# Two written-out orders of one kernel: the front's list and the round's list of an S4 convolution block

## The chip, the cores and the metric

One core of a Trainium2 chip. The metric is the device time in microseconds of one execution, the median of several.

## The reference

One block of a model on x of 2048 rows and 640 channels, all in float32. The reference, cut to what is computed:

```python
mod = (silu(c) @ w_mod).reshape(c.shape[0], 6, 1, -1)
sa, ca, ga, sb, cb, gb = (mod[:, 0], mod[:, 1], mod[:, 2], mod[:, 3], mod[:, 4], mod[:, 5])
h = layernorm(x) * (1 + ca) + sa
# A: state space convolution, per channel d, N = 128 complex states, L = 2048
P = exp(dt * A)[:, :, None] ** l
K = einsum("dn,dnl,dn->dl", Cc, P, dt * Bc).real
y = irfft(rfft(h, 2 * L) * rfft(K, 2 * L))[:L] + h * D
x = x + ga * y
h = layernorm(x) * (1 + cb) + sb
x = x + gb * ((silu(h @ w1) * (h @ w3)) @ w2)
```

So there are three parts: six modulation vectors from a small matrix product, a long convolution per channel whose kernel K must first be generated, and a gated MLP with a hidden width of 1728.

## The kernel before

The convolution is done as a Fourier transform of two stages, all products on TensorE. The 640 channels are worked in 40 **steps** of 16 channels to generate K and in 5 blocks of 128 channels to convolve; a block has eight groups of frequencies, 40 groups in all, and a word of the convolution with number k works on group k - 10 (LAG = 10), ten steps behind the generation.

The program up to the MLP has three pieces. The **front** (loop in lines 1001 to 1037) runs once over the list FRONT (lines 967 to 993). The **rounds** (loop from line 1054) run 13 times over the list ROUND (lines 1046 to 1052) with the step numbers raised by 4 each time; a word that was done before, in the front or in an earlier round, or that lies outside the steps, is skipped (do, line 918). The **tail** (loop from line 1073) does the last convolution groups, then the MLP follows, bound by TensorE.

A word of a list stands for one operation or a few, and every engine issues its instructions in the order of the words: the wrapper InOrder and keep hold the program order on each engine, and on SP's DMA queue (Qo) in the front. An engine whose next word must wait does nothing else. The words:

- PH: phases on GpSimd (turns, line 571, and a shift, line 575; in the front the shift is a word of its own, PI). AB, CO, SI: absolute value, cosine and sine of the phases, ScalarE.
- PA: two products into PSUM tile pa (line 546), XA: the exponential of it, ScalarE. PQ: four small products into tile pq (line 557), XQ: the exponential of it, ScalarE. In the rounds PA and PQ use the same PSUM bank, B; in the front each names A or B behind a stroke.
- E1, E2, A1, A2: products of exponentials with cosines and sines on VectorE (lines 598, 601, 605, 609). kg: 64 products that sum over the states (line 619). K: its eviction with a scale, VectorE (lines 626, 627). pt: first Fourier stage of K (line 638). uk: its copy to SBUF, ScalarE.
- st: second Fourier stage of a convolution group (line 677, bank A in the rounds). kc: a copy of half of it by ScalarE. T and Y: complex product and sums on VectorE (lines 694, 695, 701, 702). iv: first inverse stage (line 730). zt: every second one is copied by ScalarE and stored to memory.
- In the front: ms, mp, mc, mv (early) and qs, qp, qc, qv (late) are the modulation: sums on TensorE, a copy by VectorE (tile part), a turn on TensorE, columns by VectorE (modT, cols). z and d with a letter or figure prepare the states' parameters. s1 to s4 make the shift of the layernorm, g1 to g3 the gate. ls, lg, lv, ln: sums, power, bias and application of a layernorm to one of 16 row tiles (ln on ScalarE). um: first Fourier stage of such a tile, TensorE. ua, ub: its two evictions, on ScalarE where the word ends in /s (four small products more on TensorE then), else on VectorE. us: the store of it, from one of two buffers. xl, wl, wg, ul: loads, issued by SP.

A figure behind a stroke is the number of **idle products** (warm, line 252) on the identity, written ahead of the word's own products into the same PSUM tile; each has two records in the trace. They keep TensorE busy and compute nothing that is used. Because they write into the word's own tile, they wait until its bank is free. SETS (line 965) says which words need another table of ScalarE's functions; the loop puts the load of a table ahead of the first such word.

```python
def warm(t, n):
    out = t if len(t.shape) == 2 else t[:, 0] if t.shape[2] >= P else t[:, :P // t.shape[2]]
    for _ in range(n):
        Po.matmul(out[:, :P] if len(out.shape) == 2 else out, ident, ident, start=True, stop=True)
```

Of the kernel before, what the change touches and what calls it, by code (L numbers as in the profile page):

```python
# [116 lines left out]
def tile_kernel(ctx: ExitStack, tc: tile.TileContext, a):  # L117
# [4 lines left out]
    us = dram.tile([2, 2, NA, NB, D // 2], F32, name="us")  # L122
# [45 lines left out]
    s1 = kp.tile([P, 2, P], F32, name="s1")  # L168
# [4 lines left out]
    sc = kp.tile([P, KD], F32, name="sc")  # L173
    cT = kp.tile([P, KD], F32, name="cT")
    uk = kp.tile([P, 3, NA, DC], F32, name="uk")
# [11 lines left out]
    r2 = once([P, NA, NB], F32R, "r2")  # L187
    r1 = once([P, NA, NA], F32R, "r1")
    sel = once([P, NA], F32R, "sel")
# [46 lines left out]
    d0 = slice(0, DC)  # L236
    d1 = slice(DC, D)
# [126 lines left out]
    wg = {}  # L364
# [554 lines left out]
    wl = {}  # L919
# [15 lines left out]
    def of(p, name, *args):  # L935
# [29 lines left out]
    SETS = {"x0": 1, "z4": 1, "d5": 1, "XA": 1, "XQ": 1, "zI": 2, "d9": 2, "CO": 2, "SI": 2}  # L965

    FRONT = (
# [24 lines left out]
    ).split()  # L992

    for j in range(4):
# [46 lines left out]
    for i in range(1, 4):  # L1041
# [2 lines left out]
    xp = None  # L1044

    ROUND = (
# [5 lines left out]
    ).split()  # L1052
    in_order[0] = True
    for rnd in range(NS // EB + 3):
# [715 lines left out]
```

## Time and profile before

| | |
|---|---|
| median of 3 runs | 924.53 us (922.68 to 925.52) |
| the profiled execution's own time | 923.54 us |
| its span | 921.7 us, 21031 instructions |
| busy: TensorE, VectorE, ScalarE, GpSimd | 888.2, 699.3, 548.9, 259.6 us |
| front | about 0 to 129.65 us |
| rounds | about 129.65 to 320 us |
| tail of the convolution | about 320 to 367 us |
| MLP | about 367 us to the end |

Times in rows are microseconds from the span's start. PE is TensorE's matmul, PEld its weight load, DVE VectorE, ACT ScalarE, POOL GpSimd, SP the engine that issues most DMAs. A line number is that of the kernel's code, but operations that go through a helper all have the helper's line (L111, L146, L149, L152); there the tile's name tells which word it is. A row of a timeline gives start, duration, engine, line, operation and tiles; a bracket at its end gives the idle time just ahead of it and what ended that. A group row ends in busy time and mean duration, then the idle time ahead of its members and its releaser.

### The profile page before, as it was taken

How to read it: one execution, taken by the hardware profiler on the slowest of the kernel's cores; microseconds unless marked ns; L12 is line 12 of the kernel's file. 1: busy time of each engine (PE TensorE's matmuls, PEld its weight loads, DVE VectorE, ACT ScalarE, POOL GpSimd, SP SyncE). 2: the span in 40 equal slices, each digit the busy share in tenths (PEclk: the TensorE clock that was granted, in tenths of full speed). 3: DMA queues.
4: the chain of work that ended last, by engine and by line, in shares of the span. 5: the costliest groups of instructions: out<-in, count | busy, mean ns of one | idle time of the engine just before them, and what ended most of it. 6: DMA issues, size and time to landing. Idle time of an engine off the chain costs nothing.

```text
span 921.7 us, 21031 instructions
## 1 busy us (share of the span) xinstructions
PE 888.2 (96%) x8461; PEld 693.3 (75%) x8461; DVE 699.3 (76%) x1240; ACT 548.9 (60%) x811; POOL 259.6 (28%) x274
## 2 busy tenths in 40 slices
PE   5999899999999999999999999999999999999998
PEld 3776566677777767688888887778888888888886
DVE  6799888999999978777666665686976666664665
ACT  4799899999999834564334323566543333333432
POOL 3633455454455312132222201221522222100000
PEclk9999999999999999999999999999999999999999
DMA  8755889656666898942131117964322211113452
GB/s 255 238 203 195 258 242 228 168 161 168 165 157 156 215 259 255 262 176 86 58 115 57 58 49 230 284 223 143 100 65 71 81 58 58 58 29 100 146 176 106
DMA packets 109212, 140.87 MB, mean 153 GB/s; under 512 B 20092, under 2 KB 67452, under 8 KB 109116
## 3 DMA queue, kind: packets, MB, share of 16 engines
q1 hardware_dynamic: 103756, 130.30, 48.0%
q0 software_dynamic: 2048, 7.34, 2.3%
q10 hardware_dynamic: 3312, 1.90, 0.7%
q8 instruction: 66, 1.08, 0.5%
q14 instruction: 30, 0.25, 0.1%
HBM read 107.98 MB, written 31.52 MB: 151 GB/s over the span
## 4 chain that ended last, share of the span: by engine, by line
PE 74%; ACT 12%; DVE 9%; issue 2%; DMA 2%; SPq 0%; DVEq 0%; ACTq 0%
PE ps L111 59%; PE p L677 4%; ACT A L146 3%; ACT ph L146 2%; ACT cs L146 2%; PE pz L730 2%; DVE E L598 2%; PE pm L111 2%; ACT L146 2%; PE pt L638 1%; PE pa L111 1%; DVE uk L111 1%; PE pu L111 1%; PE pq L557 1%; ACT kc L149 1%
## 5 line engine op out<-in xcount | busy, mean ns | idle before, releaser
L111 DVE TENSOR_TENSOR s<-ps,s 128x512 f32<-128x512 f32 x138 | 94.9, 687 | 79.7 <-PE ps L111 79.3
L571 POOL TENSOR_TENSOR ph<-thi,iota 128x1024 int32<-128x1024 int32 x40 | 85.9, 2149 | 143.5 <-DVE A L609 95.4
L111 DVE TENSOR_TENSOR gl<-rw,gh 128x640 fp32r<-128x640 f32 x86 | 77.4, 900 | 62.1 <-ACT gh L111 62.1
L111 ACT CAST gh<-rw 128x640 fp32r<-128x640 f32 x86 | 62.5, 727 | 100.2 <-PE ps L111 60.5
L111 POOL TENSOR_TENSOR S<-rw 128x256 f32<-128x256 f32 x46 | 35.9, 782 | 190.6 <-DVE S0l L111 164.4
L111 PE MATMUL ps<-gh,uh 128*128 128x512 f32 x224 | 87.5, 391 | 0.0
L111 PE MATMUL ps<-gl,uh 128*128 128x512 f32 x224 | 87.2, 389 | 0.0
L677 PE MATMUL p<-uk,s 128*64 128x256 f32 x640 | 77.9, 385 | 7.1 <-DVE Y L702 2.3
L111 PE MATMUL ps<-xA,gh 128*128 128x512 f32 x270 | 84.1, 392 | 0.0
L111 PE MATMUL ps<-gh,ul 128*128 128x512 f32 x208 | 81.1, 390 | 0.0
L677 PEld LDWEIGHTS p<-uk,s 128*64 128x64 f32 x640 | 44.6, 136 | 29.5 <-DVE Y L702 3.4
L111 PEld LDWEIGHTS ps<-xA,gh 128*128 128x128 f32 x270 | 50.2, 188 | 12.2 <-ACT gh L111 0.6
L111 PE MATMUL ps<-xA,gl 128*128 128x512 f32 x135 | 52.6, 390 | 0.0
L605 DVE TENSOR_TENSOR A<-A,ph 128x1024 f32<-128x1024 f32 x40 | 51.9, 1297 | 0.0
L598 DVE TENSOR_TENSOR E<-A,cs 128x1024 f32<-128x1024 f32 x40 | 50.1, 1253 | 0.6 <-ACT A L146 0.6
L111 ACT ACTIVATE s<-ps 128x512 f32<-128x512 f32 (+1 forms) x33 | 19.6, 595 | 49.2 <-PE ps L111 47.9
L111 PEld LDWEIGHTS ps<-gl,uh 128*128 128x128 f32 x224 | 42.1, 188 | 9.0
L111 PEld LDWEIGHTS ps<-gh,uh 128*128 128x128 f32 x224 | 42.0, 188 | 8.8
L111 PEld LDWEIGHTS ps<-gh,ul 128*128 128x128 f32 x208 | 39.0, 188 | 8.4
L575 POOL TENSOR_TENSOR ph<-ph,phi 128x512 int32<-128x512 int32 x40 | 44.5, 1114 | 2.5
L730 PE MATMUL pz<-Y,i 64*128 64x128 f32 x640 | 44.4, 278 | 0.3 <-DVE Y L701 0.3
L730 PEld LDWEIGHTS pz<-Y,i 64*128 64x128 f32 x640 | 38.9, 187 | 6.8 <-issue 5.8
(257 smaller groups left out, 2292.9 us busy)
## 6 DMA issues: line engine op xcount, KB each, us to landing
rw<-in_w_dram SPq DMA_DIRECT2D x52, 320.0 KB
us<-u SPq DMA_DIRECT2D x16, 640.0 KB
s<-in_s_dram SPq DMA_DIRECT2D x40, 256.0 KB
i<-in_i_dram SPq DMA_DIRECT2D x40, 256.0 KB
rw<-in_wg_dram SPq DMA_DIRECT2D x31, 320.0 KB
rw<-in_wu_dram SPq DMA_DIRECT2D x28, 320.0 KB
uk<-us SPq DMA_DIRECT2D x32, 256.0 KB
zs<-zt SPq DMA_DIRECT2D x16, 512.0 KB
```

What stands on the lines that cost most here:

```text
L111: ins = fn(*args, **kw)
L146: return tc.keep_in_program_order(S.activation(*args, **kw))
L149: return tc.keep_in_program_order(S.copy(out, in_))
L557: keep(PE.matmul(pQ[s][:, rr, :256], w[r, t, :], bc(sel[r, js], 2, NA) if i else r1[r, js, :], start=(i == 0), stop=(i == 1), tile_positio ...
L571: keep(G.tensor_tensor(p, bc(thi[:, s * SD:s * SD + SD], 2, NPH), bc(iota, 1, SD), op=OP.mult))
L575: keep(G.tensor_tensor(p[:, :, :NA], p[:, :, :NA], bc(phi[:, s * SD:s * SD + SD], 2, NA), op=OP.add))
L598: keep(V.tensor_tensor(EC[s][:, :, 1:3, :], AA[s][:, :, 1:3, :], mid(cs[s]), op=OP.mult))
L605: keep(V.tensor_tensor(A[:, :, 1:3, :], A[:, :, 1:3, :], mid(ph[s]), op=OP.mult))
L638: keep(PE.matmul(pt[c * 64:c * 64 + 64, g, :], kk[:, g, :], s1[:, c, :], start=True, stop=True, tile_position=(0, c * 64)))
L677: keep(PE.matmul(p2[par * 64:par * 64 + 64, pi, c, :], s2[:, pi * 2 + par, c * 64:c * 64 + 64], uk[:, 0:kn + 1:kn, f, :], start=True, stop ...
L730: ins = keep(PE.matmul(pz[:, par, (g % 2) * 2 + pi, :], i1[r, pi, c, :], Y[r, pi, c, :], start=(c == 0), stop=(c == 1), tile_position=(par ...
```

## The change

The front's list gets another order of the same 427 words, with other numbers of idle products (138 for 124 in all), and ub+13 ends in /s now. The round's list gets another order of the same 86 words: E1, kc, kg, T and a sine, with iv and pt, stand at its head, the numbers of its words shift by up to a round accordingly, and idle products stand ahead of other words (8 in a steady round for 5; in all rounds 61 are run for 37). Every word is still done once; nothing else differs. The diff, cut in the front's list:

```diff
@@ -965,30 +965,29 @@
     FRONT = (
...
-        "wg+0 xl+4 zD/1 lv+1 SI+1 wg+1 zE mp+4 mc+3 PA+3/B/7 XA+2 XA+3 mc+4 d0 mv+3 mv+4 s1 PQ+0/A/1 ms+5 "
-        "s2/1 PI+2 ln+1 mp+5 ln+0 xl+6 mc+5 s4 wg+2 ms+6/1 d1 s3 PQ+1/B/1 XQ+0 E1+0 ls+4 um+0/A/1 ls+5 XQ+1 "
-        "ua+0/s ub+0/s um+1/B mv+5 E1+1 ub+1 xl+7 E2+0 PA+4/A/5 d2 ln+2 ua+1 ln+3 PQ+3/B/3 lg+2 XA+4 d3 dC "
-        "us+0 ls+6 ms+7 ls+7 um+2/A mp+6 ua+2 mc+6 lg+3 ub+2/s XQ+3 PQ+2/A/3 um+3/B xl+8 lv+2 ln+5 AB+2 us+1 "
...
-        "ua+12/s pt+2 SI+6 A1+5 uk+2 ub+12 us+12 K+4 um+13/B/2 ub+13 ua+13 ln+15 E2+5 ln+14 A1+6 wl+0 CO+7 "
-        "pt+4/6 PH+8 uk+4 A2+5 um+14/A/1 E2+6 PI+8 us+13 ub+14 wl+1 ua+14 kg+5/2 K+5 PA+8/A/1 PH+9 A2+6 "
-        "um+15/B kg+6/1 wl+2 ua+15 AB+8 SI+7 PH+10 XA+8 qs+0 qp+0 CO+8 pt+3 ub+15 PI+9 qc+0 PA+9/B/4 K+6 SI+8 "
-        "AB+9 E1+7 PQ+8/A/1 qv+0 A1+7 XA+9 qs+1 E2+7 PI+10 XQ+8 AB+10 qp+1 E1+8 PA+10/A/1 qc+1 uk+3 PQ+9/B "
-        "A2+7 XQ+9 E2+8 PH+11 pt+5 qv+1 wl+3 wl+4 XA+10 qs+2 qp+2 kg+7/4 qc+2 A1+8 PI+11 CO+9 CO+10 us+15 "
-        "AB+11 A2+8 qv+2 uk+5 CO+11 PA+11/B E1+9 qs+3 K+7 us+14 pt+7/1 PH+12 qp+3 qc+3 ul+0 qv+3 SI+10 E2+9 "
-        "SI+11 kg+8 qs+4 K+8 PQ+10/A SI+9 uk+7 PI+12 qp+4 A1+9 A2+9 pt+6 XQ+10 qc+4 XA+11 PQ+11/B uk+6 qv+4 "
-        "XQ+11 "
...
+        "x0 r2 z1 sc ld2 z2 z5 z3 z7 zF z8 zG zH z4 zI zK zJ PH+0 PI+0 ms+0/8 mp+0 ms+1 mc+0 mv+0 z9 mp+1 zA "
...
+        "wg+1 zE PA+2/A/1 lv+1 SI+1 XA+2 mc+4 mc+3 ln+2 PA+3/B/4 PI+3 XA+3 mv+3 PQ+0/A/2 XQ+0 ln+1 mv+4 xl+4 s1 "
+        "ms+5 mp+5 s2/1 mc+5 PQ+1/B/1 d1 s4 ln+3 ln+0 ms+6/1 s3 um+0/A/1 ls+4 d0 E1+0 XQ+1 ls+5 um+1/B ua+0/s "
+        "ub+0/s E2+0 d3 PA+4/A/5 mv+5 E1+1 ub+1 d2 xl+7 PQ+3/B/4 lg+2 ua+1 dC us+0 PI+2 um+2/A ls+6 ls+7 lg+3 "
+        "mp+6 ms+7 XA+4 ua+2 mc+6 xl+8 XQ+3 PQ+2/B/3 um+3/B/1 ub+2/s lv+2 A2+0 d6 ln+5 ls+8 us+1 d4 xl+9 lv+3 "
...
+        "us+12 ln+14 wl+0 PH+8 um+13/B ln+15 A1+5 ub+13/s PI+8 ua+13 E2+5 A1+6 AB+8 CO+8 A2+5 pt+4/7 um+14/B/4 "
+        "E2+6 uk+4 PH+9 ub+14 kg+5/3 us+13 ua+14 wl+1 K+5 A2+6 PA+8/B SI+7 um+15/A ua+15 wl+2 ub+15 kg+6/1 PH+10 "
+        "XA+8 qs+0 qp+0 pt+3 PI+9 SI+8 qc+0 PA+9/B AB+9 K+6 XA+9 E1+7 PQ+8/A/4 qv+0 A1+7 qs+1 E2+7 qp+1 PI+10 "
+        "XQ+8 PH+11 E1+8 PI+11 uk+3 AB+10 PA+10/A/1 PQ+9/B A2+7 E2+8 pt+5 wl+3 wl+4 qc+1 qv+1 XA+10 XQ+9 qs+2 "
+        "kg+7/3 A1+8 qp+2 CO+10 CO+9 A2+8 uk+5 qc+2 AB+11 us+15 qv+2 CO+11 PQ+10/A PA+11/B qs+3 E1+9 SI+10 PH+12 "
+        "K+7 pt+7/1 qp+3 qc+3 SI+11 kg+8 qv+3 E2+9 SI+9 qs+4 uk+7 XQ+10 A1+9 pt+6/2 qp+4 A2+9 XA+11 qc+4 uk+6 "
+        "PQ+11/B qv+4 PI+12 K+8 XQ+11 us+14 ul+0 "
@@ -1044,11 +1043,11 @@
     ROUND = (
-        "AB+8 Y+6 K+5 PQ+7/1 SI+7 CO+8 SI+8 iv+5 E2+6 st+7 A1+6 XQ+7 uk+4 PH+9 PA+8 pt+5/1 E1+7 kc+7 A2+6 PH+10 "
-        "XA+8 zt+5 PA+9 XA+9 kg+6 PQ+8 uk+5 E2+7 XQ+8 iv+6 PQ+9 T+7 Y+7 K+6 E1+8 AB+9 iv+7 XQ+9 AB+10 PA+10 st+8 "
-        "A1+7 E2+8 XA+10 zt+7 kc+8 A2+8 PQ+10 A2+7 pt+6 XQ+10 uk+6 PA+11 PH+11 T+8 XA+11 kg+7 SI+9 Y+8 st+9 kc+9 "
-        "K+7 pt+7 CO+9 A1+8 kg+8/2 SI+10 T+9 uk+7 Y+9 K+8 PH+12 CO+10 E1+9 AB+11 st+10 iv+8 CO+11 E2+9 kc+10 "
-        "A1+9 pt+8 A2+9 E1+10 kg+9/1 T+10 "
+        "iv+5 kg+5/1 E1+6 kc+6 T+6 pt+4 SI+6 PQ+7 SI+8 Y+6 K+5 CO+8 A1+6 E2+6 XQ+7 E1+7 A2+6 PH+10 uk+4 st+7 "
+        "kc+7 PA+8/1 XA+8 pt+5/2 PA+9 kg+6 PQ+8 zt+5 XA+9 uk+5 T+7 XQ+8 Y+7 iv+6 PQ+9 PH+11 E2+7 K+6 AB+9 "
+        "iv+7 XQ+9 E1+8 PA+10 A2+7 AB+10 XA+10 st+8 zt+7 PQ+10 kc+8 pt+6 PA+11 E2+8 XQ+10 uk+6 XA+11 A1+7 "
+        "A2+8 T+8 kg+7 st+9 SI+9 kc+9 Y+8 AB+11 A1+8 K+7 T+9 kg+8/2 pt+7 PH+12 K+8 CO+9 CO+11 uk+7 iv+8 SI+11 "
+        "Y+9 CO+10 PH+13 E1+9 st+10/2 AB+12 E2+9 A2+9 A1+9 "
     ).split()
```

## Rows read from the trace of the kernel before

**Rows 1.** Windows by stage: length, busy (instructions) of PE, PEld, DVE, ACT, POOL; clock, DMA share, GB/s.
```profile
0.00:36.66 36.66, 25.04 (x203) 18.95 (x203) 23.07 (x69) 21.94 (x32) 18.19 (x19) 1.00 0.89 273
36.66:129.65 92.99, 87.02 (x1497) 61.44 (x1498) 85.04 (x165) 85.92 (x109) 39.28 (x39) 0.98 0.64 216
...
163.20:320.00 156.80, 149.29 (x2891) 112.31 (x2889) 150.07 (x240) 153.12 (x191) 77.27 (x56) 1.00 0.66 173
...
367.00:921.00 554.00, 550.29 (x2599) 444.70 (x2598) 373.38 (x645) 237.08 (x410) 100.20 (x139) 1.00 0.38 117
```

**Rows 2.** The page's part 4, the chain that ended last, by engine.
```profile
PE 74%; ACT 12%; DVE 9%; issue 2%; DMA 2%; SPq 0%; DVEq 0%; ACTq 0%
```

**Rows 3.** Timeline of ACT in steady rounds: start, duration, instruction.
```profile
181.65 1.05 ACT L146 ACTIVATE cs<-ph 128x1024 f32<-128x1024 int32 x1
182.73 1.06 ACT L146 ACTIVATE cs<-cs 128x1024 f32<-128x1024 f32 x1
...
189.37 0.60 ACT L146 ACTIVATE A<-pq 128x512 f32<-128x512 f32 x1
...
190.81 1.06 ACT L146 ACTIVATE A<-pa 128x1024 f32<-128x1024 f32 x1
...
192.61 1.09 ACT L146 ACTIVATE A<-pa 128x1024 f32<-128x1024 f32 x1
```

**Rows 4.** Timeline of PE in steady rounds (matmuls on ident are idle products).
```profile
178.51 0.71 PE L111 MATMUL pk<-ident 128*128 128x128 f32 x4
...
190.02 0.50 PE L546 MATMUL pa<-r,la 64*128 64x512 f32 x2
190.50 0.49 PE L111 MATMUL pt<-ident 128*128 128x128 f32 x2
190.92 1.09 PE L638 MATMUL pt<-s,K 128*64 128x128 f32 x16
191.94 0.50 PE L546 MATMUL pa<-r,la 64*128 64x512 f32 x2
```

**Rows 5.** Timeline of DVE in one round: A1+16, T+17 [its wait], A1+17.
```profile
176.16 1.68 DVE L605 TENSOR_TENSOR A<-A,ph 128x1024 f32<-128x1024 f32 x1
178.45 0.69 DVE L694 TENSOR_TENSOR T<-p,kc 128x512 f32<-128x512 f32 x1 [0.61 <-ACT kc L149]
...
182.85 1.22 DVE L605 TENSOR_TENSOR A<-A,ph 128x1024 f32<-128x1024 f32 x1
```

**Rows 6.** Timeline of POOL in the same round: phase turns (L571) and a shift (L575).
```profile
158.64 2.75 POOL L571 TENSOR_TENSOR ph<-thi,iota 128x1024 int32<-128x1024 int32 x1 [4.34 <-DVE A L609]
...
175.71 1.05 POOL L575 TENSOR_TENSOR ph<-ph,phi 128x512 int32<-128x512 int32 x1
177.99 1.90 POOL L571 TENSOR_TENSOR ph<-thi,iota 128x1024 int32<-128x1024 int32 x1 [1.23 <-ACT ph L146]
```

**Rows 7.** One window at the start of the front's second stretch, columns as rows 1.
```profile
34.81:48.44 13.63, 12.42 (x152) 8.60 (x152) 12.42 (x27) 8.36 (x14) 5.27 (x12) 0.87 0.43 150
```

**Rows 8.** Timeline of DVE in the front: ua+2 and ua+15, each with its wait.
```profile
47.97 0.82 DVE L111 TENSOR_TENSOR u<-pu,shift 128x640 f32<-128x640 f32 x1 [0.70 <-ACT uk L146]
...
106.73 0.82 DVE L111 TENSOR_TENSOR u<-pu,shift 128x640 f32<-128x640 f32 x1 [1.79 <-DMA us<-u]
```

**Rows 9.** Groups of DVE from 104 to 130 us: busy, mean ns, idle before, releaser.
```profile
L111 DVE COPY part<-pm 128x384 f32<-128x384 f32 x5 | 2.8, 556 | 2.6 <-PE pm L111 2.5
...
L111 DVE COPY modT<-pm 128x3 f32<-128x3 f32 (+1 forms) x5 | 0.8, 155 | 1.6 <-PE pm L111 1.6
```

**Rows 10.** Timeline of ACT in the first two rounds: kc+10 [its wait] and XA+12.
```profile
131.58 0.58 ACT L149 COPY kc<-p 128x512 f32<-128x512 f32 x1 [1.34 <-PE p L677]
...
138.71 1.02 ACT L146 ACTIVATE A<-pa 128x1024 f32<-128x1024 f32 x1
```

**Rows 11.** Timelines of DVE and of PE in the tail: T+40 and stage 2 of step 42.
```profile
329.87 0.69 DVE L694 TENSOR_TENSOR T<-p,kc 128x512 f32<-128x512 f32 x1 [1.59 <-ACT kc L149]
...
334.88 1.95 PE L677 MATMUL p<-uk,s 128*64 128x256 f32 x16
```

23 rows, old and new, of the table FRONT are left out of this document.

## The prediction, made before the changed kernel ran

> **What bounds the kernel now.** I read the stages first [rows 1]. From 367 us on, TensorE is busy 550.29 of 554.00 us; the change touches no word there, so that stage only starts earlier or later. Before it, no engine is full. In the steady rounds (163.20 to 320.00) ScalarE is busy 153.12 of 156.80 us, VectorE 150.07, TensorE 149.29; in the front's second stretch (36.66 to 129.65) the three stand at 85.92, 85.04 and 87.02 of 92.99. So the two lists are a lock step of three queues in fixed order: a gain is a wait that goes, a loss is one that comes, and the busy sums move little. The chain of waits [rows 2] says the same of the whole: TensorE 74%, most of it the last stage, ScalarE 12%, VectorE 9%.
>
> Then I read each engine in order of time. The stage from 163.20, where the slow exponential of step 15 starts, holds six rounds of four steps, 156.80 / 6 = 26.13 us each, and the next begins with XQ+19 at 189.37 [rows 3]. What ends last in a round is mostly ScalarE, free 0.6 us a round by rows 1.
>
> **The round's list.** It issues the same 86 words, so the same work on each engine; its three additions are idle products. A steady round goes from 5 to 8: one ahead of PA+16 that was not there, a second one ahead of pt+13, two ahead of st+18, less the one of PQ+15. (Steps as in the round from 163.20; those timed below lie one round, 4 steps, later.)
>
> The idle of PA. PA and PQ share one PSUM bank. XQ+19 reads it from 189.37; PA+20 starts at 190.02 and takes 0.50 [rows 4], while ScalarE does two copies and then wants PA's result at 190.81 [rows 3]. An idle costs 0.42 start to start (190.50 to 190.92). It writes into the same bank, so it can't run early: PA would start at 190.44 and end at 190.94, 0.13 too late. The second idle of pt adds 0.22 (a pair takes 0.71, one 0.49 [rows 4]): PA+21 starts 0.42 + 0.22 later, at 192.58, ends at 193.08, and XA+21 starts there in place of 192.61 [rows 3]: 0.47 late in all. The next products for that bank follow it, so nothing takes it back.
>
> The two idles of st+18 wait for T+17 to leave bank A. Between T+17 and the copy that wants st+18, VectorE's list has K, Y, E1, E2, A2 and A1, some 5 us, while idles and stage 2 take 0.7 + 1.95 [rows 4, 11]: hidden, with 2 us to spare; were that cover gone, 0.64 a round. The idle of kg+13 stands at the head, where VectorE is behind with K: hidden likewise, as was the idle of PQ+15 that goes.
>
> The cosine. AB+18 is followed at once by CO+18, on the same buffer; that pair takes 1.08 start to start (181.65 to 182.73), where two unlike neighbours take 1.80, 0.90 each (190.81 to 192.61) [rows 3]. The new order puts other words between. AB reads integers, so I take -0.13 a round, less than the whole 0.18.
>
> GpSimd and VectorE. The turns at 158.64 took 2.75 us, those at 177.99 took 1.90; A1+16 took 1.68 us beside the phase shift that starts at 175.71, where A1+17 took 1.22 alone [rows 5, 6]: 0.46 lost. The new list releases PH two to four places elsewhere, beside E2+15, A1+16 and A1+14; I take 0.10 more a round, a fifth of one such meeting.
>
> Moved with their words: st issues the load of its table and, for odd groups, of u; iv issues a load, zt a store (all on SP); PH and kg sit on GpSimd's and TensorE's queues, and the last kg on GpSimd's too, with its loads. Loads go into three buffers ahead of use, and the DMA share of the stage is 0.66 [rows 1]: nothing.
>
> Sum: 0.47 - 0.13 + 0.10 = 0.44 a round, times six = **+2.6**. Bounds: -0.13 x 6 = -0.8 if all idles hide; three idles in the open, 3 x 0.42 = 1.26, give +7.6.
>
> **The front's list.** Same 427 words, 13 table loads, 14 more idles (124 to 138), and one eviction, ub+13, from VectorE to ScalarE. Up to 36.66 the loads set the pace (DMA share 0.89, each engine busy 25 us or less [rows 1]), and they are issued in nearly the same order: nothing there.
>
> Start of the stretch: of 13.63 us ScalarE is busy 8.36, VectorE 12.42 [rows 7]; ScalarE's waits have layernorm applies queued behind them. The new order puts ln+2 and ln+1 ahead of s4, and ln+3 just behind it, so ScalarE does two or three of them in its waits. VectorE, with 1.21 free there, can't follow as far: I take the 0.70 ahead of ua+2 [rows 8]. **-0.7**.
>
> ub+13: an eviction, 0.82 on VectorE like the one of rows 8. **-0.8**. ScalarE gets a copy and TensorE four small products; ScalarE has 7.07 us free in the stretch [rows 1] and 1.34 behind it [rows 10]: nothing.
>
> us+13: ua+15 waits 1.79 for a store to land [rows 8], since its buffer is one of two, and SP issues that store behind the weight load wl+0. The new list has the load right behind us+12, and VectorE gets to ub+13 sooner: I take **-1.4** of the 1.79; bounds 0, the DMA engines being busy anyway, and -1.8.
>
> The late modulation: VectorE waits 2.5 us for its sums and 1.6 for the turned columns [rows 9]. ub+15 now stands ahead of qp+0 and A1+8 ahead of qp+2, filling two of these; but qp+1 and qv+3 lose the words in front of them. I cost it at 0; half of the 4.1, 2.0, is the bound either way.
>
> End: kc+10 waits 1.34 for stage 2 [rows 10]; the new first round puts PH+13 and AB+12 there and E1+10 later: **-0.4**. The idles that came stand where TensorE has waits (6 us free in the stretch): nothing, unless one stands in front of a late product.
>
> Sum -0.7 - 0.8 - 1.4 - 0.4 = **-3.3** at XA+12, now 138.71 [rows 10]. Bounds -0.8 (ub+13 alone) and -5.3 (with the 2.0).
>
> **The tail.** T+40 waits 1.59 for its copy [rows 11]; the new order has stage 2 of step 40 earlier by about one A1, 1.2 us, but the next copy waits for the bank. I take **-0.9** at st+42, now 334.88. Bounds -1.6 and +0.5 (an idle more).
>
> **Sum:** -3.3 + 2.6 - 0.9 = -1.6. The profiled execution took 923.54 (span 921.7) and would take 921.9; it stands 1.0 under the median of the three runs, 924.53, which gives **922.9**.
>
> **A rule weighed.** A1+16 starts at 176.16, while a shift runs (175.71 to 176.76), and takes 0.46 more than A1 alone [rows 5, 6]; the second one lost about what the first had left, 0.60. The Trainium skill, "SBUF — State Buffer", section "SBUF: two separate sides", says that GpSimd and VectorE share a pair of ports as an exclusive lock, that whoever starts second waits for the whole instruction, and that a VectorE operation with two SBUF inputs takes part in it. By that the trace agrees, and it speaks against this change: products that read PSUM (T, Y, K) would be spared, E and A not, and PH moves to E and A. By the page a product that starts just behind the turns would lose all of them, 1.9 us (no row shows such a start); four of these a round in place of the 0.1 are about +7.5 a round, and the sum would be near 968.
>
> **Rivals.**
> A: the idles cost nothing, because XA+16 and XA+17 are late for another reason or TensorE has run ahead. For it: TensorE is free 1.25 us a round [rows 1]. Against: ScalarE leaves the bank 0.65 before PA starts, and the idle can only start there. -3.3 - 0.8 - 0.9 = -5.0: 919.5. Chance 0.32.
> B (slower): GpSimd's phases fall beside wide products in all four steps of a round. 4 x 0.46 = 1.84; with the one such meeting of before taken off, +1.38 a round, +8.3 in place of +2.6, VectorE then hiding the idles. -3.3 + 8.3 - 0.9 = +4.1: 928.6. It decides from 4.2 / 6 = 0.70 us a round. For it: PH already stretches A1+16. Against: T+17 waits 0.61 after it for ScalarE [rows 5], which takes some back. Chance 0.16.
> C: the front gives back what it gains, the sums of the late modulation being late in new places (qp+1, qv+3). Only ub+13's 0.8 is left: -0.8 + 2.6 - 0.9 = +0.9: 925.4. For it: 4.1 us of such waits in rows 9. Against: ub+15 and A1+8 fill two. Chance 0.12.
> The forecast keeps 0.40.
>
> **How the numbers follow.** About 0.3% (2.8 us) is what a measurement of this kernel can tell from no change. Faster by more: nearly all of A and a seventh of the forecast, 0.35. Slower: most of B, a fifth of C, little of the forecast, 0.18. Within: 0.47. The range runs from just under A, 918.5, to just under B, 928.0; outside lie the far half of B and the far ends of A.
>
> **What would show it.** Right: XA+12 about 3.3 us before 138.71; ua+15's wait under 0.5; a round of 26.5 to 26.7; XA+21's place 0.5 later behind XQ+19; stage 2 of step 42 about 1.6 us before 334.88. A would show as a round of 26.0, B as A1 and E1 of 1.5 us or more at three or four places of a round, C as waits for pm of 5 us and more. It is wrong if the round is under 25.9 or over 27.0, or if the last stage no longer takes 554 us.

## The result, and the profile after

The changed kernel takes 925.49 us in the median (923.07 to 928.63, 22 runs), the kernel before 923.44 (22 runs): a ratio of 1.0023 with a 95% interval of 1.0014 to 1.0032, so 2.05 us slower. The forecast was 1.6 us faster: its range held the time, but the sign was wrong. On another chip the unchanged kernel of after gave 925.80 against 923.59, 1.0019 (1.0001 to 1.0036).

The two traces are compared by marks that both have: s3 (VectorE's copy of the shift's row), E1+10, XA+12, XA+39, h+47 (ScalarE's copy of tile pz 1.09 us behind kc+47; the expectation of f2 calls this mark kc+48) and the MLP's first products (ps<-idle). The table gives the first mark and then the times between marks, each the difference of two starts in the timelines; "round" is (XA+37 - XA+17) / 5. The third line is the unchanged kernel of after once more (f3).

```
              s3    to E1+10  to XA+12  to XA+39  to h+47   to MLP  to end   span   round
before       37.74    93.14     7.83     166.74     47.36   14.50   554.42  921.74  26.181
after        37.25    92.73     8.32     169.07     46.39   15.69   554.20  923.66  26.585
after, again 36.13    93.42     8.32     169.03     46.42   14.89   555.08  923.28  26.578
```

So, from before to after: -0.49 up to s3, -0.41 in the rest of the front, +0.49 in the first rounds, +2.33 in the rounds, -0.97 in the tail, +1.19 in the convolution's last groups, -0.22 in the MLP: +1.92. In the two executions of after, the stages from E1+10 to h+47 repeat within 0.04 us; the time to s3 and the MLP's differ by about one microsecond and the rest of the front by 0.69, so single spans say little and the later stages a lot.

For the front one pair is therefore not enough, and the experiments below give more traces of both lists: before's front also stands in e1, e11 and e12, after's in e2 to e6, f2 and f3. From s3 to ua+2 all of them take 9.44 or 9.45 us, and VectorE doesn't wait for ua+2; only the trace of before takes 10.23, with the wait of 0.70 [rows 8]. It is also the only one of them whose granted clock was at 1.2 GHz between s3 and ua+2, so that four microseconds there have 0.67 in the mean (first row, columns as rows 1; the second row is ua+2 in e1):

```profile
42.00:46.00 4.00, 4.00 (x34) 3.05 (x18) 3.97 (x8) 3.21 (x5) 3.92 (x9) 0.67 0.91 313
```

```profile
46.91 0.81 DVE L111 TENSOR_TENSOR u<-pu,shift 128x640 f32<-128x640 f32 x1
```

From s3 to E1+10 before's list takes 92.25, 92.26 and 92.31 us in e11, e12 and e1, 93.14 only in the trace of before; after's takes 92.73 to 93.51 in its eight. So this part of the front became 0.4 to 1.3 us longer, where the pair shows 0.41 shorter. Up to s3 it is the other way round: 37.46 to 38.48 with before's list, 35.73 to 37.25 with after's (39.91 in e6); what makes that difference is open.

The round first. The page's part 4 shows the chain moving to TensorE [rows 2 had 74%]:

```profile
PE 82%; ACT 8%; DVE 7%; issue 2%; DMA 1%; DVEq 0%
```

ScalarE in the round that answers to rows 3 (start, duration, instruction, idle before):

```profile
189.12 0.60 ACT L146 ACTIVATE A<-pq 128x512 f32<-128x512 f32 x1
...
190.97 1.02 ACT L146 ACTIVATE A<-pa 128x1024 f32<-128x1024 f32 x1 [0.26 <-PE pa L546]
...
193.07 1.02 ACT L146 ACTIVATE A<-pa 128x1024 f32<-128x1024 f32 x1 [0.17 <-PE pa L546]
```

and TensorE beside it, with the idle products of PA and pt [rows 4]:

```profile
188.13 1.95 PE L677 MATMUL p<-uk,s 128*64 128x256 f32 x16
190.01 0.49 PE L111 MATMUL pa<-ident 128*128 128x128 f32 x2
190.43 0.50 PE L546 MATMUL pa<-r,la 64*128 64x512 f32 x2
190.86 0.71 PE L111 MATMUL pt<-ident 128*128 128x128 f32 x4
191.50 1.09 PE L638 MATMUL pt<-s,K 128*64 128x128 f32 x16
192.52 0.51 PE L546 MATMUL pa<-r,la 64*128 64x512 f32 x2
```

XA+20 now waits 0.26 and XA+21 0.17 for their products, where before there was no wait; from XQ+19 to XA+21 it is 3.95 us for 3.24 [rows 3]. Every second round is like this one and takes 26.7 us; in the others the first wait is under 0.1, XQ to XA takes 3.73, and the round 26.5. The idle of PA starts at 190.01, when stage 2 ends, though XQ+19 had left the bank at 189.72: here it is TensorE's queue that it stands in, not the bank that it waits for. In the kernel before it was the same: PA+20 started at 190.02 [rows 4], when this stage 2 ended:

```profile
188.10 1.95 PE L677 MATMUL p<-uk,s 128*64 128x256 f32 x16
```

The front, VectorE's waits between 55 and 129 us:

```profile
57.60 0.83 DVE L111 TENSOR_TENSOR u<-pu,shift 128x640 f32<-128x640 f32 x1 [0.84 <-PE pu L111]
...
66.51 0.17 DVE L626 TENSOR_TENSOR pk<-pk,dz 128x4 f32<-128x4 f32 x1 [0.46 <-PE pk L619]
...
105.99 1.55 DVE L111 TENSOR_TENSOR u<-pu,shift 128x640 f32<-128x640 f32 x2 [0.64 <-DMA us<-u]
108.44 0.56 DVE L111 COPY part<-pm 128x384 f32<-128x384 f32 x1 [0.90 <-PE pm L111]
...
128.54 0.16 DVE L111 COPY modT<-pm 128x1 f32<-128x1 f32 x1 [1.07 <-PE pm L111]
```

The first two are new (ub+4 and K+1); ua+15's wait fell from 1.79 [rows 8] to 0.64; the late modulation's waits changed places (0.90, 0.56, 1.61, 1.07, together 4.1 as in rows 9; in the other seven traces of this list 4.2 to 5.2).

TensorE at the front's end, and much later at the last stage-2 group:

```profile
128.86 0.71 PE L111 MATMUL p<-ident 128*128 128x128 f32 x4
...
358.99 1.95 PE L677 MATMUL p<-uk,s 128*64 128x256 f32 x16 [1.12 <-DMA s<-in_s_dram]
```

The first row is the two idles of st+10, in front of the stage 2 that kc+10 and T+10 wait for; the second a wait that the trace of before does not have.

### The profile page after: what moved, and what is told of

Its sections match the earlier page's. It is cut to its first block, busy times and chain, and to the rows that moved or that the text cites. A ratio compares the mean times of both kernels' runs of the same rounds, so it can differ in the third digit from the quotient of the medians.

```text
span 923.7 us, 21171 instructions
## 1 busy us (share of the span) xinstructions
PE 898.7 (97%) x8545; PEld 701.2 (76%) x8545; DVE 700.8 (76%) x1239; ACT 550.7 (60%) x812; POOL 262.5 (28%) x274
## 4 chain that ended last, share of the span: by engine, by line
PE 82%; ACT 8%; DVE 7%; issue 2%; DMA 1%; DVEq 0%
PE ps L111 59%; PE p L677 6%; PE pt L638 3%; PE pz L730 3%; ACT A L146 2%; PE pk L619 2%; PE pm L111 2%; ACT cs L146 2%; PE pq L557 1%; DVE A L605 1%; DVE uk L111 1%; DMA s<-in_s_dram 1%; PE pk L111 1%; PE pa L546 1%; PE pq L111 1%
## 5 line engine op out<-in xcount | busy, mean ns | idle before, releaser
L571 POOL TENSOR_TENSOR ph<-thi,iota 128x1024 int32<-128x1024 int32 x40 | 87.2, 2181 | 142.9 <-DVE A L605 53.7
L605 DVE TENSOR_TENSOR A<-A,ph 128x1024 f32<-128x1024 f32 x40 | 54.8, 1369 | 0.5 <-ACT ph L146 0.4
L575 POOL TENSOR_TENSOR ph<-ph,phi 128x512 int32<-128x512 int32 x40 | 47.6, 1191 | 2.6
```

The costliest lines, as they stand in the source:

```text
L571: keep(G.tensor_tensor(p, bc(thi[:, s * SD:s * SD + SD], 2, NPH), bc(iota, 1, SD), op=OP.mult))
L575: keep(G.tensor_tensor(p[:, :, :NA], p[:, :, :NA], bc(phi[:, s * SD:s * SD + SD], 2, NA), op=OP.add))
L605: keep(V.tensor_tensor(A[:, :, 1:3, :], A[:, :, 1:3, :], mid(ph[s]), op=OP.mult))
```

## The experiments

**e1 and e2: one list each.** e1 has before's front and after's rounds, e2 the reverse.

> The front's list of before with the round's list of after. Theory (the loss of the after kernel arises in the rounds, from the idle products ahead of PA and the second one ahead of pt, which wait for the bank): XA+17 moves later by 0.3 to 0.5 us in each of six rounds as in the after kernel, +2.3 from XA+12 to XA+39, the tail gives back 1.0, so 0.9 to 2.5 us slower than before: 924.3 to 925.9, the upper end if the last stage-2 group again waits 1.1 us for its table. Rival 1 (the front's list brings the loss): as before, 923.4. Rival 2 (only both lists together lose): 923.4 as well, with a round of 26.13.

> The front's list of after with the round's list of before. Theory: the new front alone is 0.4 to 1.1 us ahead at XA+12 (E1+10 stands 0.89 earlier in the after trace, and the old round has no idles ahead of stage 2 of step 10, which cost 0.64 there), and the rounds keep 26.13 us: 922.3 to 923.0, below before by less than can be told surely. Rival 1 (the front's list brings the loss): 924.5 or more. Forecast of the prediction for this part alone: 3.3 us faster, 920.1.

Measured: e1 926.14 (ratio 1.0030, 1.0011 to 1.0049), e2 923.33 (0.9999, 0.9988 to 1.0010). In e1 a round takes 26.586, in e2 26.192. The rounds' list alone makes a slower kernel; the front's list alone makes none that can be told apart from before, where 3.3 us less were forecast.

**e3: without the two idles on bank B.**

```diff
-kc+7 PA+8/1 XA+8 pt+5/2 PA+9
+kc+7 PA+8 XA+8 pt+5/1 PA+9
```

> The after kernel without the idle product ahead of PA+8 of the round's list and with one for two ahead of pt+5. Theory: the steps of 0.3 to 0.5 us from XQ+15 to XA+17 in each round vanish, the round falls to 26.05 or less, and the time falls by 2.3 to 2.8 us from the after kernel's 925.5 to 922.7 to 923.2. Rival (the round is longer because GpSimd's phases or the cosines stand elsewhere): 925.5 stays, round of 26.5.

Measured: 924.69 (1.0011, 0.9997 to 1.0026), round 26.439, XA+12 to XA+39 167.89 for 169.07. Less than expected, which was a round of 26.05 or less: the waits of XA went, but only 0.15 us of a round's 0.40 with them, and something else took their place. VectorE in e3, one round:

```profile
253.20 1.93 DVE L605 TENSOR_TENSOR A<-A,ph 128x1024 f32<-128x1024 f32 x1
...
257.60 0.17 DVE L626 TENSOR_TENSOR pk<-pk,dz 128x4 f32<-128x4 f32 x1 [0.22 <-PE pk L619]
```

GpSimd and TensorE of e3 beside it:

```profile
253.00 1.04 POOL L575 TENSOR_TENSOR ph<-ph,phi 128x512 int32<-128x512 int32 x1
```

```profile
255.81 0.68 PE L111 MATMUL pk<-ident 128*128 128x128 f32 x4 [0.53 <-DVE K L627]
```

A1+28 starts 0.2 us after the shift and takes 1.93, 0.71 more than alone [rows 5]. K+27 stands behind it; the two idles of kg+28 write into the bank that K+27 reads, wait for it, and so K+28 waits for kg+28. In the kernel of after A1+28 took 1.51, because T+28 was late anyway (a wait of 0.33 for kc), and A1+24 1.72 behind a wait of 0.12. One wait hid part of the other.

**e5 and e6: the two ways out of that.** e5 is e3 with two words exchanged, e6 is the kernel of after with no idle in the rounds.

```diff
-AB+11 A1+8 K+7 T+9
+AB+11 K+7 A1+8 T+9
```

> The kernel of e3 (no idle ahead of PA, one ahead of pt) with the words A1+8 and K+7 of the round's list exchanged, so that VectorE's wide product A1 no longer starts while GpSimd's turns or shift run, as far as K's 0.6 us reach. Theory (with the idles gone, what is left of the longer round, 0.24 us, is VectorE held up by GpSimd: A1+28 took 1.93 us in e3): A1+28 takes 1.5 or less, the round falls from 26.43 to 26.1 or 26.2, XA+12 to XA+39 grows by 0.3 or less over before (e3: 1.15), and the time is 0.8 to 1.2 us below e3: 923.5 to 923.9. Rival (what is left comes from the idles ahead of kg, which delay K): round of 26.4 as in e3, 924.7.

> The after kernel with no idle product at all in the round's list. Theory: besides what e3 gained, K's wait for kg (0.22 a round) and the delay of stage 2 of step 10 (0.64 once) go; VectorE held up by GpSimd stays, so the round is 26.2 to 26.4 and the time 923.6 to 924.3. Rival 1 (the idles hold the granted clock up): the clock falls under 1.00 somewhere between 163 and 320 us and the time is 926 or more. Rival 2 (the idles are the whole loss of the rounds): round of 26.0, 922.8.

Measured: e5 924.08 (0.9997, 0.9983 to 1.0011), round 26.100; e6 921.96 (0.9981, 0.9964 to 0.9998), round 26.098. Both take the last 0.3 us off: e5 because K+27 comes before the long A1, e6, where A1+28 still takes 1.93, because no idle waits behind K+27. So neither the long A1 (e6) nor the idles of kg with A1 behind K (e5) cost anything alone; that it is kg's idles among those that e6 took out is read from the rows of e3, not tried by itself. Theory and rival of e5 were both half right, and of e6's guesses rival 2 came nearest.

**e4: without the two idles of st+10.**

> The after kernel without the two idle products ahead of st+10 of the round's list. Theory: in the steady rounds they are hidden behind VectorE's work, but the first ones, ahead of stage 2 of step 10, delay kc+10 and T+10 by 0.64: T+10 moves from 132.11 to 131.5 or a little less, and 0.5 to 0.9 us are gained in all: 924.6 to 925.0. Rival 1 (hidden there as well): 925.5, no change. Rival 2 (in the open in each round): 0.64 a round, 4 us faster, 921.5.

Measured: 924.48 (1.0008, 0.9992 to 1.0025). E1+10 to XA+12 takes 7.84 again, as before: the first ones cost 0.48. The round is 26.476, and from XA+17 on all rounds are alike, so in the steady rounds they were not quite hidden either: they made every second round 0.2 us longer, 0.11 in the mean. From XA+12 to XA+39, though, only 0.27 us are gained (168.80 for 169.07).

**e11 and e12: the old rounds, and the new order, without idles.**

> The kernel before with no idle product in its round's list. Theory (the old list's five idles a round were hidden, ScalarE setting the pace; the one ahead of pt left 0.13 us to spare): round of 26.13 as before, 923.2 to 923.8. Rival 1 (idles cost there too): round of 26.0 or less and 0.8 us or more below before. Rival 2 (the clock falls): 925 or more.

> The front's list of before with the round's list of after without idles. Theory (the new order of the rounds as such gains the 0.08 us a round of e6 and T+10's part at the start): 922.3 to 923.2, 2.5 to 3.5 below e1, which has the same order with its idles. Rival (the order as such costs, too): 924 or more, round over 26.2.

Measured: e11 923.92 (1.0007, 0.9997 to 1.0017), round 26.177: in the steady rounds the five idles of the old list were free. (XA+12 to XA+39 takes 168.00 for 166.74 all the same, because of the first rounds; more on that with e9.) e12 921.31 (0.9982, 0.9968 to 0.9996), round 26.089, E1+10 to XA+12 7.52: the new order as such gains 0.09 us a round. Its idles, not its order, made it slow.

**e7 and f4: fewer idles in the front** (no word with more than it had in before's list: 106 in all for 138; the same kernel twice, f4 on the chip of f1 to f3).

> The after kernel, where no word of the front's list has more idle products than it had in the list of before (106 in all for 138). Theory (idles ahead of um+5 and um+6 make the evictions of um+5 and K+1 late: VectorE waits 0.84 and 0.46 us for them in the after trace): both waits go or fall under 0.4, E1+10 stands 0.5 to 1.1 us nearer to s3 than in the after trace (131.4 - 0.89 - 37.25 = 92.7 there), and the time is 924.5 to 925.0. Rival (the idles run in TensorE's free time): the same waits, 925.5. Second rival: with fewer idles the granted clock falls once more in the front, and 926 or more.

> The kernel of e7 (fewer front idles, the rounds as in after), beside the after kernel on one chip. Theory (the front's added idles cost 1.8 us, by the traces): 1.3 to 2.3 us below the after kernel of this chip. Rival (the clock or the stages behind take it back): within 0.6 of it.

Measured: s3 to E1+10 takes 90.95 in e7 and 90.94 in f4, for 92.73 and 93.42 of after (the 131.4 in the expectation is 130.88 in the trace). In time: e7 923.75 (1.0010, 0.9985 to 1.0034), f4 924.57 (1.0004, 0.9979 to 1.0029), 1.2 us under the kernel of after on its chip; the intervals are too wide for the 1.8 to 2.5 of the traces to be told in the times. Up to K+1 it is 28.08 and 27.89 us for 29.25 or 29.26 in all eight traces of after's list, and 27.8 in e1, e11 and e12: the added idles cost 1.2 to 1.4 us by there. Most of the rest comes at kg+6, ahead of K+6 and of the late sums, where after's list has a stop of TensorE that f4 has not (see f3). In f4 VectorE's two new waits are gone and the one for qp+0, 0.90 in after and 1.97 in f3, is 0.41:

```profile
55.81 0.82 DVE L111 TENSOR_TENSOR u<-pu,shift 128x640 f32<-128x640 f32 x1
...
64.17 0.16 DVE L626 TENSOR_TENSOR pk<-pk,dz 128x4 f32<-128x4 f32 x1
...
105.56 0.56 DVE L111 COPY part<-pm 128x384 f32<-128x384 f32 x1 [0.41 <-PE pm L111]
```

**f1 and f3: one word's idles, and the base.** f1 has PQ+4/A/4 for PQ+4/A/9.

> The after kernel with 4 for 9 idle products ahead of PQ+4 in the front's list, nothing else. Theory (the first of the front's new waits, VectorE's 0.84 us for um+4's product ahead of ub+4, comes from these five idles, 5 x 0.22 = 1.1 us of TensorE's queue): that wait falls under 0.3, K+1's 0.46 stays, and s3 to E1+10 shortens by 0.5 to 0.9 from 92.7. Rival (um+4 is late for another reason): wait of 0.6 or more, nothing gained.

> The after kernel unchanged, as the base of the three others on one chip. Theory: 1.5 to 2.6 us over before, front's waits of 0.84, 0.46, 0.64, 0.90, 1.07 as in the first trace, a round of 26.58. For the table's wait of the last group both are open: 1.1 us again (then it belongs to the change), or none (then it was that execution's).

Measured: f1 925.61 (1.0014, 0.9996 to 1.0032). The wait ahead of ub+4 (0.83 in f3) is gone, K+1's 0.46 stays, s3 to K+1 takes 28.56 for 29.25: 0.69 us from five idles, and s3 to E1+10 92.58 for 93.42. f3 also shows what the rest of the front's loss is. TensorE there:

```profile
104.88 0.28 PE L619 MATMUL pk<-A 128*32 128x64 f32 x4
106.64 0.25 PE L619 MATMUL pk<-A 128*32 128x64 f32 x2 [1.48 <-issue]
...
107.90 1.09 PE L638 MATMUL pt<-s,K 128*64 128x128 f32 x16
```

In the middle of kg+6 TensorE stops for 1.48 us and the profile shows nothing that it waited for; the sums of qs+0 stand behind, and qp+0 waits 1.97 for them. This stop is taken up in the last section.

**e8: ub+13 back on VectorE.**

> The after kernel with the eviction ub+13 on VectorE again (no /s). Theory (what VectorE saves there it waits for again a few words on, for a store to land ahead of ua+15 or for the late sums): ua+15's wait of 0.64 us falls by most of the 0.8 that the eviction costs, E1+10 moves by 0.3 or less, 925.5 stays within 0.4. Forecast's own term: 0.8 us slower, 926.3.

Measured: 926.96 (1.0016, 0.9988 to 1.0044), too wide to tell. The trace tells more: s3 to ua+15 takes 68.84 for 68.74 in after. VectorE in e8:

```profile
104.99 1.56 DVE L111 TENSOR_TENSOR u<-pu,shift 128x640 f32<-128x640 f32 x2
106.99 0.56 DVE L111 COPY part<-pm 128x384 f32<-128x384 f32 x1 [0.44 <-PE pm L111]
```

ua+15, the first of the pair, hardly waits for its store now. The 0.8 us that ub+13 costs VectorE are 0.1 at ua+15. (E1+10 then stands 92.57 behind s3, not later than in after: e8 has no stop in kg+6.)

**f2: the last table.** The MLP's first two weight tiles are asked for one group later.

> The after kernel with the first two weight tiles of the MLP (320 KB each) asked for one group later, so that they no longer stand ahead of the last stage-2 table in SP's queue. Theory (that table came 1.1 us late in the after trace because the DMA engines were full and these two stood in front): no wait for s ahead of the last stage 2, kc+48 to the MLP's first product takes 14.5 in place of 15.7, unless the weights then come late for the MLP. Rival (a chance of that execution): the after kernel without this edit, on the same chip, shows no such wait either.

Measured: 926.19 (1.0028, 1.0012 to 1.0043); h+47 to the MLP takes 14.80, in f3, without the edit, 14.89, and neither waits for the table. The rival holds: 1.1 of the 1.92 us in the first pair of traces were that execution's (0.2 in e1, e6 and e8, none in the others). What made the table late there is open.

**e9 and e10: what the runs point to.** e9 has the front of e7 and no idles in the rounds, e10 also A1 behind K.

> The after kernel with the fewer idles of e7 in the front and none in the rounds, as in e6. Theory (the two losses are idles that wait for a bank or stand in front of a late product, and they are separate): E1+10 stands 1.5 to 2.2 us nearer to s3 than in the after trace, the round takes 26.1, T+10 loses no 0.64, and the time is 920.5 to 922.0, below both kernels. Rival (the granted clock falls more often without these idles): 924 or more, with the clock under 0.99 in the mean.

> The kernel of e9 with A1+8 and K+7 of the round's list exchanged as in e5. Theory (with the idles of kg gone, K+27's delay by the long A1 reaches nobody, since T+29 waits for ScalarE): T+29's wait grows from 0.3 to 0.8 us, the round stays 26.1, the time that of e9 within 0.4. Rival (VectorE held up by GpSimd still costs): round of 25.8 or less and 1.5 us and more below e9.

Measured: e9 921.10 (0.9971, 0.9951 to 0.9992), e10 919.90 (0.9968, 0.9940 to 0.9995), both below the kernel before on their chip, by 0.3%; the kernel of after was above it on the two chips that ran it. The round is 26.088 and 26.087: as the theory said, A1 behind K brings nothing once no idle waits for K, because T+29 waits for ScalarE instead, 0.82 us in e10:

```profile
252.14 1.39 DVE L605 TENSOR_TENSOR A<-A,ph 128x1024 f32<-128x1024 f32 x1
254.34 0.69 DVE L694 TENSOR_TENSOR T<-p,kc 128x512 f32<-128x512 f32 x1 [0.82 <-ACT kc L149]
```

The steady stage of e10, columns as rows 1:

```profile
163.20:320.00 156.80, 140.58 (x2828) 104.13 (x2830) 149.42 (x241) 150.95 (x190) 80.36 (x56) 1.00 0.66 173
```

TensorE is busy 140.58 us there for 149.29 in rows 1, and the granted clock is still 1.00, 2.4 GHz: in this stage the idle products were not what kept it up. In the first rounds (129.65 to 163.20) it is different: three of the five traces without idles there (e6, e9, e11) have 0.95 in the mean, 3.4 us of it at 1.2 GHz, and XA+12 to XA+39 takes 167.27, 167.31 and 168.00 there; e10 and e12 stay at 1.00 and take 166.14 and 166.15 (e11 has before's order, 166.74 with its idles). In those three TensorE had stopped without a releaser for 1.1 to 1.3 us ahead of a stage 2, before the clock fell; in e10 it stopped as long and the clock stayed. So idles may be worth 1.1 to 1.3 us in the first rounds of some executions; whether it is their lack that makes these stops is open. A front without idles was not tried.

## Why the prediction was wrong

**The rounds came out as forecast, in part by luck:** +2.33 us for +2.6, 0.40 us a round for 0.44. XA+21 was late by 0.49 us in every second round and 0.71 in the others, for 0.47 forecast; but the idle of PA stood in TensorE's queue behind stage 2, where the prediction has it waiting for the bank. What the trace of before could not say is that a second limit lay just below: with the two idles gone (e3) only 0.15 us a round came back, since VectorE and the idles of kg then set the pace, and 0.11 was the idles of st, costed at nothing behind "2 us to spare" (e4). The price was right as a sum, its parts were not: the idles ahead of PA and pt alone were priced at 0.47, and the order alone, priced at -0.03 (the cosine's -0.13 and GpSimd's +0.10), gained 0.09 (e12 beside e11).

**The tail was right:** -0.97 for -0.9, and f1, f2, f3 and e8 repeat it within 0.03. In e1, with the same rounds, a stop of TensorE (0.77 us at 312.64, no releaser shown) took it back.

**The front failed:** -3.3 was forecast at XA+12; -0.41 came in the pair, of which -0.49 lies ahead of s3, where nothing was forecast. The step that failed is the sentence that the added idles stand where TensorE has waits and cost nothing "unless one stands in front of a late product". They stood in front of three: um+4 (0.69 us, f1), kg+1 (K+1's 0.46, gone in f4), and stage 2 of step 10, where -0.4 was forecast and +0.49 came (e4 gives 0.48 back). At K+1 after's list is 1.5 us behind before's of e1, e11 and e12. Behind that, and ahead of the sums that qp+0 waits for, stands the stop in kg+6, which is there with after's idles and not with e7's, nor in e8. TensorE was free 6 us in the stretch, but each of those words was awaited, and busy share does not say which gaps lie ahead of an awaited word. Reading what follows each lengthened word on TensorE's queue, and who waits for it, would have shown them: 0.22 us of queue an idle, of which f1's five brought 0.69 of 1.1 into the open.

The gains failed too. ua+2's -0.7 was not there to take: its wait of 0.70 stands in the one trace that the forecast was read from and in none of e1, e11 and e12, with the same list. ub+13's -0.8 was not there (e8): VectorE then waits for the store of us+13, which the forecast treated as a gain of its own. us+13's own wait fell by 1.15 in the pair, 1.4 forecast (0.24 to 1.03 are left in the eight traces, of 1.69 to 1.79). At ua+15, by which these three should have brought 2.9 us, after's list stands 68.35 to 69.14 us behind s3 and before's 68.10 to 68.12 (68.98 in the trace of before): by these marks the idles cost as much as all gains brought, or more. The late modulation at 0 was right in the pair, 4.1 us of waits for 4.1, by luck: f3 has 5.2, with the stop in front. Rival C, that the front gives back what it gains, gave 925.4, and 925.49 came; its mechanism (late sums) is part of it.

**Outside the sum:** the last table's wait, +1.1 in the profiled pair, is no part of the change by f2 and f3. The medians' 2.05 us are then the rounds' 2.33 less the tail's 0.97, the 0.49 of the first rounds, and a front that gives nothing (e2's ratio of 0.9999): 1.85.

**The rule weighed** held in kind: in e3 A1+28 started 0.2 us into a shift of 1.04 and lost 0.71 of the 0.84 that the shift had left. By the Trainium skill, "SBUF — State Buffer", section "SBUF: two separate sides", the second one waits for the whole instruction; the trace agrees here too, as nearly as 0.71 to 0.84. But rival B, which rested on it, did not decide: in the steady rounds GpSimd lengthened three products a round before (E1 to 1.39, A1 to 1.68, E2 to 0.79) and three after (E1 and two of A1), by 0.8 us a round in all in both traces, and A1's longer time came out only when other waits were gone.

## What to carry to other kernels

An idle product costs its time when the word behind it is awaited; if that word's bank is still being read, it waits for the bank and can't run in the gap (the idles of kg in e3). Price it by the queue behind it, not by the engine's free time. When two engines run in lock step, take one cost away and look at the round again before believing its price; here e3 gave back 0.15 us a round where XA's waits were 0.23 and 0.43 in turn, and e5 and e6, two unlike edits, the same rest. Where one resource runs short behind another (ub+13 and the store of us+13), two gains in the same stretch are one. And look for a wait in a second execution before putting it in a sum: the 0.70 of ua+2 was one execution's.

## What the runs showed of the hardware

TensorE's stop without a releaser was not expected. In the eight traces with after's front as it is, and in f1, it stands in the middle of kg+6, near 107 us, 0.78 to 1.55 us long; in e8, which has four small products fewer ahead of it, in the four traces with e7's fewer idles, and in the four with before's list there is none at that place. In f3 a block of 16 KB of the instruction queue starts in the window 104 to 105, while the DMA engines are full (window view of DMA queues, packets, MB, share):

```profile
q1 hardware_dynamic: 278, 0.28, 101.8%
q8 instruction: 1, 0.02, 7.9%
```

In each of the nine traces with the stop such a block began 2.4 to 2.7 us before TensorE went on. That fits code arriving late, at a place that moves with the number of products ahead of it; it was not tried by itself, and stays an inference. Two things stand against a simple rule: such a block begins near there without a stop, too (103.90 in e7, 103.04 in e8, 106.04 in before), and of fourteen more stops of this kind over 0.4 us in e1, e3 to e6 and e9 to e11 (0.60 to 1.27 us, most of them near 310) nine come 2.3 to 2.7 us behind a block and five do not. For this kernel it is worth up to 1.5 us, more than most edits of an order.

The granted clock differs between the lists as well. All ten traces with after's front, as it is or with one word changed (e8, f1), have 6.8 or 10.2 us at 1.2 GHz between 14 and 26 us; the four with before's list and the four with e7's have none there. The row of after that answers to the first of rows 1:

```profile
0.00:36.66 36.66, 26.14 (x208) 20.61 (x208) 24.46 (x70) 22.92 (x33) 17.13 (x18) 0.86 0.90 273
```

No loss is seen from it: s3 does not come later in nine of these traces, and e2, which has it, takes 923.33. The tenth, e6, has a second such stretch from 32.9 to 39.7 us, and there s3 is late (39.91).
